# A spectral layer and an ELU network in one kernel: first-layer PSUM by the bank, the B step on 128 rows, and a bias moved

## The chip, the cores and the metric

The kernel runs on one core of one Trainium2 chip. The metric is device time in microseconds (us), the median of several executions. Engines: TensorE (PE in the profile; PEld is its weight load), VectorE (DVE), ScalarE (ACT), GpSimd (POOL) and SyncE (SP), which here only issues transfers.

## The reference

Eight sequences of 3008 rows and 256 columns go through a real Fourier transform along the rows, a complex linear map, a soft threshold, the inverse transform, and then a two-layer network:

```
X = rfft(x, axis=1)                          # Xr, Xi
Yr = Xr @ w_r - Xi @ w_i + b_r
Yi = Xr @ w_i + Xi @ w_r + b_i
Y  = sign(Y) * max(|Y| - 0.01, 0)            # each of Yr, Yi
y  = irfft(Yr + 1j*Yi)                       # 24064 rows x 256
h  = y @ w_in                                # 256 -> 2048
g  = h if h > 0 else exp(min(h, 0)) - 1
out = g @ w_out                              # 2048 -> 256, float32
```

## The kernel before

**The transform.** 3008 = 47 x 64. The forward transform is two sets of matmuls, A (`unit_A`, matrix M1) and X (`unit_X`, matrix M2), the inverse is B (`unit_B`, matrix M3) and Y (`unit_Y`, matrix M4). Between X and B stands M (`unit_M`): the complex map in three real products, its bias and the soft threshold. A sequence has 6 A units, 8 X, 12 M (q from 0 to 5, i 0 and 1), 6 B and 8 Y units. Between A and X, and between B and Y, the data go through DRAM to change their layout (tiles DA, Z, DB, Bs). Each unit of A, X, B and Y fills a pair of PSUM banks (pool psF, one pair) and is copied out by ScalarE or VectorE; M has two banks of its own pool (psM), which takes the place of psF where it is asked for.

**M.** In sequences 2 to 7, k1 (256 columns) is copied to SBUF by VectorE (L295), ps plus that copy is written to yb (L296), and GpSimd adds both biases (L301), clips (L302) and subtracts (L303) into the tile Y: 128 rows, two values of pp, 512 columns. The rows of Y are (s, n2) with s 0 or 1 and 64 values of n2; its columns are (c, d), c the real or imaginary part.

**B.** For each of the two pp, the sum over (c, n2) is made by two matmuls of 64 rows, c 0 and 1, once for each s: eight matmuls of 64 rows and 256 columns a unit.

**The network.** `front(i)` is step i: four matmuls (two halves s of 512 columns, two of the contraction) into the bank pair `hps`, pool psH with two pairs, and ScalarE's Exp of it into Et. `elu` and `finish_elu` make gT, in one of three ways: on "act" steps ScalarE does Relu and Exp of both banks in one pass each (L1024, L1025) and VectorE one pass of 1024 columns (L1048); on "pool" steps ScalarE does Exp by halves (L1022), GpSimd min by halves (L1059) and VectorE L1048 by halves; on the others VectorE does both (L1061, L1050). The pass L1048 reads hps and so gives it back. `back(i)` two steps later multiplies gT by w_out: eight matmuls of 256 columns (L1080) into `ps_o`; every eighth step the sum is copied to osb (L1092) and stored.

**The order.** It is written out by hand. A sequence of the network has 47 steps. `plan(b)` puts the units of the next sequences (A of b+2; X, M, B and the first two Y of b+1; the rest of Y of b) into the steps of b, one unit before a step's front (list f0) or behind it (f1, mostly transfers). `on_act` names the steps of the "act" way, besides all M steps. In the first plan, X starts at step 10. Before step 0 stands a start of some 50 us that does the first sequence's transform with functions of its own (`first_M`, `turn_B`, `split_B`).

All transfers but those of x and w_out are issued by SP, in the order of the program; an issue waits for its operands at the head of that queue.

Of the kernel before, what the change touches and what calls it, by code (L numbers as in the profile page):

```python
# [29 lines left out]
def kernel(  # L30
# [28 lines left out]
    M3 = constp.tile([P, K1 // 2, 2, P], BF16, name="M3")  # L59
# [6 lines left out]
    bias_p = constp.tile([P, 2 * D], BF16, name="bias_p")  # L66
# [10 lines left out]
    space = constp.tile([P, 384], BF16, name="space")  # L77
# [26 lines left out]
    Y_of = {}  # L104
    Bz_of = {}
# [122 lines left out]
    def sum_of(dt, ch):  # L228

        return XS[:, 3 * dt + ch] if 3 * dt + ch < 5 else busy[:]  # L230

    def three_weights(c, dt):

        v, r = (w[:, dt, D * c : D * c + D] for w in (wcat_s, wcat_r))
        a, b_ = (r, v) if c else (v, r)
        nc.gpsimd.tensor_tensor(v, a, b_, ALU.subtract)

    mps_of = {}

    def m_group(b, q, i, ps, biased=False):  # L240
        XT = XT_of[b]
        o = (2 * q + i) * P
        todo = [(c, dt) for c in range(2) for dt in range(2)]
        if b == 0:
            todo.sort(key=lambda z: z[1])
        for c, dt in todo:
            nc.tensor.matmul(  # L247
                ps, lhsT=XT[:, dt, c, o : o + P], rhs=(wcat_r, wcat_s)[c][:, dt, :],
                start=(not biased and (c, dt) == (0, 0)), stop=((c, dt) == (1, 1)),
            )  # L250
        if i == 0:
            Y_of[b, q] = wk3.tile([P, 2, 2 * D], BF16, name="Y", tag="Y")
        if biased:
            yb = ps
        else:
            yb = wk3.tile([P, 2 * D], F32, name="yb", tag="yb")[:]
            nc.vector.tensor_tensor(yb, ps, bias_bc[:], ALU.add)
        if (b, q, i) == (0, 2, 0):
            clip = late3.tile([P, 2 * D], F32, name="gT", tag="gT")
        else:  # L260
            clip = wk2.tile([P, 2 * D], F32, name="clip", tag="clip")
        return yb, clip

    def unit_M(b, q, i):
# [8 lines left out]
        if i == 0:  # L273
            Y_of[b, q] = wk3.tile([P, 2, 2 * D], BF16, name="Y", tag="Y")
# [20 lines left out]
        evac(yb[:, D : 2 * D], k1[:, 0:D], True)  # L295
# [5 lines left out]
        nc.gpsimd.tensor_tensor(yb[:], yb[:], bias_bc[:], ALU.add)  # L301
# [61 lines left out]

    def unit_B(b, v, alone=False, on_dve=False, all_dve=False):
# [5 lines left out]
        Bz, Y = Bz_of[b, v // 2], Y_of.pop((b, v))  # L370
        ps = unit_ps("bps", alone)
        for pp in range(2):
            for c in range(2):
                for s in range(2):
                    nc.tensor.matmul(  # L375
                        ps[:, s, pp * D : pp * D + D],
                        lhsT=M3[s * N2 : s * N2 + N2, 2 * v + pp, c, :],
                        rhs=Y[s * N2 : s * N2 + N2, pp, c * D : c * D + D],
                        start=(c == 0), stop=(c == 1),
                    )  # L380
# [8 lines left out]
        if alone:  # L389
            k0 = 4 * v  # L390
            nc.sync.dma_start(
                DB_of[b][k0 : k0 + 4].rearrange("k p d -> p k d"), Bz[:, o : o + 4, :]
            )
        elif b == 1 and v > 3:
# [19 lines left out]
    def split_B(v, ps, on_dve=(False, True), by_half=False):  # L414
# [8 lines left out]
        def half(pp):  # L423
            for c in range(2):
                for s in range(2):
                    nc.tensor.matmul(
                        ps[s][:, pp * D : pp * D + D],
                        lhsT=M3[s * N2 : s * N2 + N2, 2 * v + pp, c, :],
# [25 lines left out]
    def turn_B(v, ts=(0, 1), ps=None, on_dve=False):  # L454
# [11 lines left out]
        for pp in range(2):  # L466
            for dt in ts:
                for c in range(2):
                    for s in range(2):
# [7 lines left out]
                            rhs=M3[s * N2 : s * N2 + N2, 2 * v + pp, c, :].rearrange(  # L477
# [76 lines left out]

    nc.vector.memset(bias_p[:], 0.0)
# [274 lines left out]
    XS = sump.tile([P, 5, 512], BF16, name="XS")  # L830
# [60 lines left out]
    for o, src, sc, bi in ((1, w3, TURN, 0.0), (0, a3, -TURN, hpi[:])):  # L891
        if o == 0:
            nc.scalar.activation(a3[:], w3[:], AF.Abs)
        nc.scalar.activation(
            M3[:, :, 0, o * N2 : o * N2 + N2], src[:], AF.Sin, bias=bi, scale=sc
# [4 lines left out]
        M3[:, :, 1, 0:N2], M3[:, :, 0, N2:P], 2.0, sgb, ALU.mult, ALU.mult  # L900
    )
    nc.vector.scalar_tensor_tensor(
        M3[:, :, 1, N2:P], M3[:, :, 0, 0:N2], -2.0, sgb, ALU.mult, ALU.mult
# [82 lines left out]
    def front(i, third, on_act, halves):  # L986
        blk, fp = divmod(i, NPAIR)
        early = i < FILL
        if early:
# [10 lines left out]
        if i == PER // NPAIR * NPAIR:  # L1000
            todo.sort(key=lambda z: z[2][0])
        Et = late3.tile([P, 2, TB], F32, name="Et", tag="Et")
        E_ = Et[:]
        for s, ft, (b, t0, c0, c1) in todo:
            for dt in range(2):
                nc.tensor.matmul(  # L1006
                    hps[s][:, c0:c1] if early else hps[:, s, c0:c1],
# [4 lines left out]
            if early and (dt, c1) == (1, TB):  # L1012
                nc.scalar.activation(E_[:, s], hps[s][:], AF.Exp)
        if early:
            return hps, Et
        if i == n - 1:
            for h in range(2):
                t = slice(TB // 2 * h, TB // 2 * h + TB // 2)
                nc.scalar.activation(E_[:, :, t], hps[:, :, t], AF.Exp)
        elif halves:  # L1020
            for s in range(2):
                nc.scalar.activation(E_[:, s], hps[:, s], AF.Exp)  # L1022
        elif on_act:
            nc.scalar.activation(E_, hps[:], AF.Relu, scale=-1.0)  # L1024
            nc.scalar.activation(E_, E_, AF.Exp, scale=-1.0)  # L1025
        else:
            nc.scalar.activation(E_, hps[:], AF.Exp)  # L1027
# [3 lines left out]
    np_all = (slice(0, P), slice(0, 2), slice(0, TB))  # L1031

    def parts(i):

        if i == n - 1:
            return [
                (slice(0, P), slice(0, 2), slice(h, h + TB // 2)) for h in (0, TB // 2)
            ]
        return [(slice(0, P), s, slice(0, TB)) for s in range(2)]

    def finish_elu():
        for i, hps, Et, whole, halves in late_elu:
            gT = late3.tile([P, 2, TB], F32R, name="gT", tag="gT")
            for s in parts(i) if halves else (np_all,):
                h = hps[s[1]][:] if i < FILL else hps[s]
                o, e = gT[s], Et[s]
# [7 lines left out]
    def elu(i, hps, Et, on_pool, on_act):  # L1054

        E_ = Et[:]
        if on_pool:
            for s in parts(i):
                nc.gpsimd.tensor_scalar(E_[s], E_[s], 1.0, 0.0, ALU.min, ALU.max)  # L1059
        elif not on_act:  # L1060
            nc.vector.tensor_scalar(E_, E_, 1.0, -1.0, ALU.min, ALU.add)  # L1061
        late_elu.append((i, hps, Et, on_pool or on_act, on_pool))
# [47 lines left out]
    def plan(b):  # L1110
# [10 lines left out]
        ]  # L1121
        if n1 < B:
            if b:
                lead, xs = 0, (3, 6, 9) if b < 3 else (3, 8, 13)
# [6 lines left out]
                if b < 3:  # L1131
                    seq += [("y", 4)] + M(0) + M(1) + [("y", 5), ("B", 0)]
                else:
                    seq += M(0) + [("y", 4)] + M(1) + [("y", 5), ("B", 0)]
                seq += M(2) + [("y", 6), ("B", 1)] + M(3) + [("y", 7), ("B", 2)]
                on_act = [("X", 4), ("X", 7), ("B", 3)] + [("y", u) for u in range(5, 8)]
                if b < 3:
                    on_act += [("A", 0)]
                    seq += M(4) + [("B", 3)] + M(5) + [("A", 0), ("B", 4), ("B", 5)]
                    seq += [("A", u) for u in range(1, 6)]  # L1140
                else:
                    on_act += [("y", 4), ("B", 4)]
                    seq += M(4) + [("B", 3), ("A", 0)] + M(5) + [("B", 4), ("A", 1), ("B", 5)]
                    seq += [("A", u) for u in range(2, 6)] + [None] * (3 if n2 == B else 2)
                seq += [("n", 0), ("n", 1)]
            else:
                lead, seq = FILL, (
                    [u for u in mid if u[0] != "A"]
                    + [("A", 0), ("A", 1), ("A", 2), ("n", 0), ("n", 1)]
                    + [("A", u) for u in range(3, 6)]  # L1150
                )
# [3 lines left out]
        for t, u in enumerate(seq, lead):  # L1155
# [14 lines left out]
            elif u[0] == "A":  # L1170
                if n2 < B:
                    f0[t].append(put("A", n2, u[1]))
            else:
                f0[t].append(put(u[0], n1, *u[1:]))
            if u == ("B", 5):
                f1[t + (b > 0 and n2 < B)] += [
                    (load_Bs, (n1, w, 0, 4 * K1 - 16 * (b == w == 0))) for w in range(4)
                ]
# [3 lines left out]
        if b == 0:  # L1182
# [24 lines left out]
    for i in range(n + LAG):  # L1207
        if i == FILL:
# [3 lines left out]
                    name="psH", bufs=2, space=bass.MemoryType.PSUM, reuse_waits="tile"  # L1212
# [6 lines left out]
        elif i < n:  # L1219
# [16 lines left out]
            h = front(i, third, on_act, pooled)  # L1236
        finish_elu()
        if i < n:
# [12 lines left out]
            if i == n - 2:  # L1251
                early_h = front(n - 1, True, False, True)
# [36 lines left out]
```

## Time and profile before

| what | us |
|---|---|
| runs | 895.38, 894.95, 894.54; median 894.95 |
| the profiled execution: its span, first to last instruction (the page gives no other time of it) | 903.9 |
| mean granted TensorE clock, share of full speed | 0.948 |
| GpSimd's additions of the biases, L301 | 92.3 in 72 instructions |
| B's matmuls, L375 | 336, mean record 274 ns |
| first-layer matmuls of 512 columns, L1006 into hps | 1240, mean record 390 ns |

The profiled execution is 1.0% longer than the median of the runs. Records of matmuls overlap, as each lasts until its result is out; how fast TensorE goes is read from one start to the next. Idle time of other engines costs nothing unless TensorE then waits for them.

### The profile page before, as it was taken

What the parts mean: (1) busy time and instruction counts of PE and PEld (TensorE: products, weight loads), DVE (VectorE), ACT (ScalarE), POOL (GpSimd) and SP (SyncE); (2) the same over time, 40 slices, a digit from 0 to 9 for tenths busy, and PEclk for the clock granted to TensorE, in tenths of its full rate; (3) what the DMA queues carried; (4) which work ended last, traced back from release to release, by engine and by line L of the source; (5) the groups of instructions that cost most, each with busy time, mean ns of one, the idle gap of its engine ahead of it and who ended that gap; (6) DMA issues with size and microseconds to landing.
All of it is one profiled execution on the core that took longest, in us unless ns stands there. A gap on an engine that the chain in (4) does not pass through costs nothing.

```text
span 903.9 us, 18292 instructions
## 1 busy us (share of the span) xinstructions
PE 891.3 (99%) x6917; PEld 675.2 (75%) x6917; DVE 679.6 (75%) x969; ACT 722.4 (80%) x1001; POOL 596.7 (66%) x806
## 2 busy tenths in 40 slices
PE   9999999999999999999999999999999999999997
PEld 3467667877788777877778777787777877777776
DVE  7788778688866887668866788677876678778776
ACT  6778778888978889798887988878887798776654
POOL 7562550788657886588756877559875697753664
PEclk9999999999999999999999999999999999999998
DMA  8996226631474115632265231643218201241111
GB/s 262 310 258 188 70 71 181 169 119 47 118 209 124 65 50 152 173 117 88 72 181 136 86 116 48 189 140 101 87 53 229 70 24 48 69 108 36 28 44 47
DMA packets 90718, 105.85 MB, mean 117 GB/s; under 512 B 5395, under 2 KB 81174, under 8 KB 87302
## 3 DMA queue, kind: packets, MB, share of 16 engines
q1 hardware_dynamic: 84278, 76.64, 30.0%
q0 software_dynamic: 5968, 27.26, 9.4%
q8 instruction: 54, 0.88, 0.4%
q10 hardware_dynamic: 384, 0.79, 0.3%
q14 instruction: 34, 0.28, 0.1%
HBM read 54.86 MB, written 49.81 MB: 116 GB/s over the span
## 4 chain that ended last, share of the span: by engine, by line
PE 90%; DVE 3%; DMA 3%; ACT 2%; POOL 1%; issue 1%; SPq 0%; DVEq 0%; ACTq 0%; POOLq 0%
PE ps_o L1080 37%; PE hps L1006 36%; PE mps L289 5%; PE bps L375 2%; PE xps L207 2%; PE yps L538 2%; PE aps L170 2%; DVE gT L1048 2%; PE mps L247 1%; DVE Bz L144 1%; DMA xt<-in_x_dram 1%; DMA Z<-DA 1%; DMA DB<-Bz 1%; PE sps L1006 1%; DMA DA<-A 0%
## 5 line engine op out<-in xcount | busy, mean ns | idle before, releaser
L1048 DVE SCALAR_TENSOR_TENSOR gT<-Et,hps 128x512 fp32r<-128x512 f32 (+1 forms) x544 | 423.7, 811 | 158.5 <-POOL Et L1059 115.4
L1080 PE MATMUL ps_o<-w_out_r,gT 128*128 128x256 f32 x3008 | 481.4, 303 | 0.0
L1080 PEld LDWEIGHTS ps_o<-w_out_r,gT 128*128 128x128 f32 x3008 | 407.7, 190 | 52.4 <-ACT osb L1092 0.5
L1059 POOL TENSOR_SCALAR Et<-Et 128x512 f32<-128x512 f32 x434 | 258.3, 614 | 223.6 <-ACT Et L1022 213.2
L1006 PE MATMUL hps<-yT,w_in_s 128*128 128x512 bf16 (+7 forms) x1688 | 388.9, 360 | 2.0 <-DVE gT L1048 1.3
L1022 ACT ACTIVATE Et<-hps 128x512 f32<-128x512 f32 x412 | 224.2, 598 | 67.8 <-PE hps L1006 63.3
L1006 PEld LDWEIGHTS <-w_in_s 128*128 128x128 bf16 x1728 | 144.7, 99 | 119.7 <-issue 21.7
L1024 ACT ACTIVATE Et<-hps 128x1024 f32<-128x1024 f32 x130 | 133.6, 1027 | 57.3 <-PE hps L1006 49.0
L1025 ACT ACTIVATE Et<-Et 128x1024 f32<-128x1024 f32 x130 | 137.4, 1057 | 4.1
L301 POOL TENSOR_TENSOR yb<-yb,bias_bc 128x512 f32<-128x512 f32 x72 | 92.3, 1282 | 9.5 <-DVE yb L296 9.4
L303 POOL TENSOR_TENSOR Y<-yb,clip 128x512 bf16<-128x512 f32 x72 | 92.6, 1286 | 6.0
L296 DVE TENSOR_TENSOR yb<-mps,yb 128x512 f32<-128x512 f32 x72 | 49.8, 692 | 7.6 <-PE hps L1006 0.5
L146 ACT CAST XT<-xps 128x768 bf16<-128x768 f32 x57 | 45.5, 799 | 9.8 <-PE xps L207 9.7
L146 ACT CAST A<-aps 128x1024 bf16<-128x1024 f32 x40 | 40.5, 1014 | 11.4 <-PE aps L170 9.9
L302 POOL TENSOR_SCALAR clip<-yb 128x512 f32<-128x512 f32 x72 | 44.2, 614 | 6.3
L289 PE MATMUL mps<-wcat_s,XT 128*128 128x256 bf16 x288 | 44.1, 277 | 0.0
L144 DVE COPY yb<-mps 128x256 f32<-128x256 f32 x72 | 30.3, 421 | 11.1 <-PE mps L289 9.7
L1050 DVE SCALAR_TENSOR_TENSOR gT<-hps,Et 128x1024 fp32r<-128x1024 f32 x29 | 35.5, 1223 | 2.4
L224 POOL TENSOR_TENSOR XS<-XT 128x512 bf16<-128x512 bf16 x30 | 34.1, 1159 | 2.1 <-ACT XT L146 1.2
L1092 DVE COPY osb<-ps_o 128x512 f32<-128x512 f32 x46 | 31.6, 686 | 1.2 <-PE ps_o L1080 0.5
L146 ACT CAST Bz<-bps 128x1024 bf16<-128x1024 f32 x32 | 31.9, 998 | 0.5 <-PE bps L375 0.4
L1027 ACT ACTIVATE Et<-hps 128x1024 f32<-128x1024 f32 x29 | 29.8, 1029 | 2.6 <-PE hps L1006 1.2
(184 smaller groups left out, 678.8 us busy)
## 6 DMA issues: line engine op xcount, KB each, us to landing
xt<-in_x_dram POOLq DMA_DIRECT2D x21, 1024.0 KB, 5.4
out_dram<-osb SPq DMA_DIRECT2D x158, 128.0 KB
Bs<-DB SPq DMA_DIRECT2D x30, 384.0 KB
DB<-Bz SPq DMA_DIRECT2D x20, 512.0 KB
DA<-A SPq DMA_DIRECT2D x19, 512.0 KB
Z<-DA SPq DMA_DIRECT2D x5, 1152.0 KB
Z<-DA SPq DMA_DIRECT2D x11, 384.0 KB
xt<-in_x_dram POOLq DMA_DIRECT2D x6, 512.0 KB, 6.0
```

The source lines that it names most:

```text
L146: nc.scalar.copy(dst, src)
L289: nc.tensor.matmul(out_, lhsT=lhs[:, dt] if lhs is not None else sum_of(dt, ch)[:, oc : oc + P], rhs=w[:, dt, :], start=(dt == 0), stop=(d ...
L296: nc.vector.tensor_tensor(yb[:].rearrange("p (c d) -> p c d", c=2), ps[:].rearrange("p (c d) -> p c d", c=2), yb[:, D : 2 * D].unsqueeze(1 ...
L301: nc.gpsimd.tensor_tensor(yb[:], yb[:], bias_bc[:], ALU.add)
L303: nc.gpsimd.tensor_tensor(Y_of[b, q][:, i, :], yb[:], clip[:], ALU.subtract)
L1006: nc.tensor.matmul(hps[s][:, c0:c1] if early else hps[:, s, c0:c1], lhsT=w_in_s[:, dt, ft * P : ft * P + P], rhs=yT_of[b][:, dt, t0 : t0 + ...
L1022: nc.scalar.activation(E_[:, s], hps[:, s], AF.Exp)
L1024: nc.scalar.activation(E_, hps[:], AF.Relu, scale=-1.0)
L1025: nc.scalar.activation(E_, E_, AF.Exp, scale=-1.0)
L1048: nc.vector.scalar_tensor_tensor(o, e, -1.0, h, ALU.add, ALU.max)
L1059: nc.gpsimd.tensor_scalar(E_[s], E_[s], 1.0, 0.0, ALU.min, ALU.max)
L1080: nc.tensor.matmul(po[q][:, i_ % 2, :], lhsT=gT[:, s, i_ * P : i_ * P + P], rhs=w_out_r[:, ft, :], start=(ft == 0 and i_ % 2 == 0), stop=( ...
```

## The change

- **First layer.** `hps` becomes two tiles of one bank each (psH: four tiles of a bank). ScalarE's and VectorE's passes L1024, L1025, L1027, L1048 and L1050 go by halves everywhere. The extra pair that idle stretches use comes from psM in place of psF, except for the last step.
- **B.** M3 is kept as two tiles M3[0], M3[1] for the start only and regrouped by four transfers into M3x with rows (c, n2) (`turn_M3`, step 6). After the second M unit of each q, four transfers of 64 rows bring Y to Yx with rows (c, n2) (`turn_Y`), and a B unit is four matmuls of 128 rows without accumulation. Y and Yx share four buffers of pool wk4.
- **M.** b_r is added in the copy of k1; `three_weights` makes b_i - b_r, and GpSimd then adds that to the second half only.
- **Ways and order.** Of the "act" steps beside M, X 4 and X 7 stay; B, Y and A steps go the "pool" way, and their copies to ScalarE. B 0 comes behind M 2, B 5 earlier or later by some steps; the four loads of Bs that follow B 5 are spread over five steps; in the first plan the A units go between the B units, and the first Y unit (n 0) stands three steps behind B 5.
- bias_p moves into a buffer of Bs, `space` shrinks.

```diff
-    M3 = constp.tile([P, K1 // 2, 2, P], BF16, name="M3")
+    M3x = constp.tile([P, K1 // 2, 2, P], BF16, name="M3x")
...
+        if c == dt == 0:
+            b_r_, b_i_ = (bias_bc[:, D * k : D * k + D] for k in range(2))
+            nc.gpsimd.tensor_tensor(b_i_, b_i_, b_r_, ALU.subtract)
...
-        evac(yb[:, D : 2 * D], k1[:, 0:D], True)
+        nc.vector.tensor_tensor(yb[:, D : 2 * D], k1[:, 0:D], bias_bc[:, 0:D], ALU.add)
...
-        nc.gpsimd.tensor_tensor(yb[:], yb[:], bias_bc[:], ALU.add)
+        nc.gpsimd.tensor_tensor(
+            yb[:, D : 2 * D], yb[:, D : 2 * D], bias_bc[:, D : 2 * D], ALU.add
+        )
...
+    def by_part(dst, of):
+        for c in range(2):
+            for s in range(2):
+                nc.sync.dma_start(dst[c * N2 : c * N2 + N2, :, s, :], of(c, s))
+    def turn_M3():
+        by_part(M3x, lambda c, s: M3[c][s * N2 : s * N2 + N2])
+    def turn_Y(b, q):
+        Y = Y_of.pop((b, q))
+        Yx_of[b, q] = Yx = wk4.tile([P, 2, 2, D], BF16, name="Yx", tag="Y")
+        by_part(Yx, lambda c, s: Y[s * N2 : s * N2 + N2, :, c * D : c * D + D])
...
         for pp in range(2):
-            for c in range(2):
-                for s in range(2):
-                    nc.tensor.matmul(
-                        ps[:, s, pp * D : pp * D + D],
-                        lhsT=M3[s * N2 : s * N2 + N2, 2 * v + pp, c, :],
-                        rhs=Y[s * N2 : s * N2 + N2, pp, c * D : c * D + D],
-                        start=(c == 0), stop=(c == 1),
-                    )
+            for s in range(2):
+                nc.tensor.matmul(
+                    ps[:, s, pp * D : pp * D + D], lhsT=M3x[:, 2 * v + pp, s, :],
+                    rhs=Yx[:, pp, s, :], start=True, stop=True,
+                )
...
+        elif last:
+            pair = last_banks("psF").tile([P, 2, TB], F32, name="hps", tag="fps")
+            hps = [pair[:, s, :] for s in range(2)]
         elif third:
-            hps = last_banks("psF").tile([P, 2, TB], F32, name="hps", tag="fps")
+            hps = two_banks(last_banks("psM"), "mps")
         else:
-            hps = psH.tile([P, 2, TB], F32, name="hps", tag="hps")
+            hps = two_banks(psH, "hps")
...
+            left[s] -= 1
+            if left[s] or last:
+                continue
+            if on_act:
+                nc.scalar.activation(Et[:, s], hps[s], AF.Relu, scale=-1.0)
+            else:
+                nc.scalar.activation(Et[:, s], hps[s], AF.Exp)
+        if on_act:
+            for s in range(2):
+                nc.scalar.activation(Et[:, s], Et[:, s], AF.Exp, scale=-1.0)
...
-                on_act = [("X", 4), ("X", 7), ("B", 3)] + [("y", u) for u in range(5, 8)]
+                on_act = [("X", 4), ("X", 7)]
...
+            if u[0] == "M" and u[2] == 1:
+                f1[t].append((turn_Y, (n1, u[1])))
             if u == ("B", 5):
-                f1[t + (b > 0 and n2 < B)] += [
-                    (load_Bs, (n1, w, 0, 4 * K1 - 16 * (b == w == 0))) for w in range(4)
-                ]
+                for w, k in enumerate((0, 2, 3, 4)):
+                    f1[t + k].append((load_Bs, (n1, w, 0, 4 * K1 - 16 * (b == w == 0))))
...
+            f1[6].append((turn_M3, ()))
...
-                    name="psH", bufs=2, space=bass.MemoryType.PSUM, reuse_waits="tile"
+                    name="psH", bufs=4, space=bass.MemoryType.PSUM, reuse_waits="tile"
```

More of the change, by code (lines that the diff above doesn't have):

```diff
@@ L104 @@
     Y_of = {}
+    Yx_of = {}
+    M3 = []
+    XS_of = []
     Bz_of = {}
@@ L228, in sum_of @@
     def sum_of(dt, ch):
-        return XS[:, 3 * dt + ch] if 3 * dt + ch < 5 else busy[:]
+        if 3 * dt + ch == 5:
+            return busy[:]
+        if not XS_of:
+            XS_of.append(sump.tile([P, 5, 512], BF16, name="XS", tag="XS"))
+        return XS_of[0][:, 3 * dt + ch]
     def three_weights(c, dt):
@@ L393, in unit_B @@
             )
-        elif b == 1 and v > 3:
+        elif b == 1 and v > 1:
             nc.sync.dma_start(
@@ L553, in idle_pe @@
             nc.tensor.matmul(ips[:], lhsT=busy[:, 0:P], rhs=busy[:], start=True, stop=True)
+    bias_p = wk4.tile([P, 2 * D], BF16, name="bias_p", tag="Bs")
     nc.vector.memset(bias_p[:], 0.0)
@@ L984, in pieces, with front @@
         return out_
-    def front(i, third, on_act, halves):
+    def front(i, third, on_act):
         blk, fp = divmod(i, NPAIR)
-        early = i < FILL
-        if early:
+        last = i == n - 1
+        if i < FILL:
             hps = two_banks((psS0, psS1)[i % 2], "sps")
+        elif last:
+            pair = last_banks("psF").tile([P, 2, TB], F32, name="hps", tag="fps")
+            hps = [pair[:, s, :] for s in range(2)]
         elif third:
-            hps = last_banks("psF").tile([P, 2, TB], F32, name="hps", tag="fps")
+            hps = two_banks(last_banks("psM"), "mps")
         else:
-            hps = psH.tile([P, 2, TB], F32, name="hps", tag="hps")
+            hps = two_banks(psH, "hps")
+        hps = [h if last else h[:] for h in hps]
         todo = []
@@ L1006, in front @@
                 nc.tensor.matmul(
-                    hps[s][:, c0:c1] if early else hps[:, s, c0:c1],
+                    hps[s][:, c0:c1],
                     lhsT=w_in_s[:, dt, ft * P : ft * P + P],
@@ L1011, in front, with parts @@
                 )
[L1012 to L1016, printed above, removed]
+            left[s] -= 1
[8 more added lines that the diff above has]
+                nc.scalar.activation(Et[:, s], Et[:, s], AF.Exp, scale=-1.0)
+        if last:
             for h in range(2):
                 t = slice(TB // 2 * h, TB // 2 * h + TB // 2)
[L1019 to L1027, printed above, removed]
+                nc.scalar.activation(Et[:, :, t], pair[:, :, t], AF.Exp)
+            hps = pair
         return hps, Et
     late_elu = []
-    np_all = (slice(0, P), slice(0, 2), slice(0, TB))
-    def parts(i):
+    def parts(i, hps, Et):
         if i == n - 1:
-            return [
-                (slice(0, P), slice(0, 2), slice(h, h + TB // 2)) for h in (0, TB // 2)
-            ]
-        return [(slice(0, P), s, slice(0, TB)) for s in range(2)]
+            for h in (0, TB // 2):
+                t = slice(h, h + TB // 2)
+                yield t, slice(0, 2), hps[:, :, t], Et[:, :, t]
+        else:
+            for s in range(2):
+                yield slice(0, TB), s, hps[s], Et[:, s]
     def finish_elu():
-        for i, hps, Et, whole, halves in late_elu:
+        for i, hps, Et, whole in late_elu:
             gT = late3.tile([P, 2, TB], F32R, name="gT", tag="gT")
-            for s in parts(i) if halves else (np_all,):
-                h = hps[s[1]][:] if i < FILL else hps[s]
-                o, e = gT[s], Et[s]
+            for t, s, h, e in parts(i, hps, Et):
+                o = gT[:, s, t]
                 if whole:
@@ L1054, in elu @@
     def elu(i, hps, Et, on_pool, on_act):
-        E_ = Et[:]
         if on_pool:
-            for s in parts(i):
-                nc.gpsimd.tensor_scalar(E_[s], E_[s], 1.0, 0.0, ALU.min, ALU.max)
+            for t, s, h, e in parts(i, hps, Et):
+                nc.gpsimd.tensor_scalar(e, e, 1.0, 0.0, ALU.min, ALU.max)
         elif not on_act:
-            nc.vector.tensor_scalar(E_, E_, 1.0, -1.0, ALU.min, ALU.add)
-        late_elu.append((i, hps, Et, on_pool or on_act, on_pool))
+            nc.vector.tensor_scalar(Et[:], Et[:], 1.0, -1.0, ALU.min, ALU.add)
+        late_elu.append((i, hps, Et, on_pool or on_act))
     def back(i, split):
```

55 lines of the change are left out of this document (25 added, 30 removed), and 8 rows, old and new, of the table mid.

## The prediction

> **What bounds the kernel now.** I read the page first: engine totals, then the chain that ended last.
>
> ```profile
> PE 891.3 (99%) x6917; PEld 675.2 (75%) x6917; DVE 679.6 (75%) x969; ACT 722.4 (80%) x1001; POOL 596.7 (66%) x806
> ...
> PE 90%; DVE 3%; DMA 3%; ACT 2%; POOL 1%; issue 1%; SPq 0%; DVEq 0%; ACTq 0%; POOLq 0%
> ...
> L301 POOL TENSOR_TENSOR yb<-yb,bias_bc 128x512 f32<-128x512 f32 x72 | 92.3, 1282 | 9.5 <-DVE yb L296 9.4
> ```
>
> TensorE is the bound, so a change pays only through what TensorE itself does or waits for. "99% busy" hides waits, because records of consecutive matmuls overlap: one of 512 columns lasts 390 ns, but starts follow at 223 ns. So I measured from start to start in the timeline of PE. A stretch with a B unit (L375) and an M unit (L289):
>
> ```profile
> 198.79 1.29 PE L1080 MATMUL ps_o<-w_out_r,gT 128*128 128x256 f32 x8
> 200.01 0.62 PE L375 MATMUL bps<-Y,M 64*128 64x256 bf16 x8
> 200.56 1.06 PE L1006 MATMUL hps<-yT,w_in_s 128*128 128x512 bf16 x4
> 201.26 1.29 PE L1080 MATMUL ps_o<-w_out_r,gT 128*128 128x256 f32 x8
> 202.39 0.39 PE L289 MATMUL mps<-wcat_r,XS 128*128 128x256 bf16 x2
> 202.62 0.61 PE L289 MATMUL mps<-wcat_s,XT 128*128 128x256 bf16 x4
> 203.07 1.06 PE L1006 MATMUL hps<-yT,w_in_s 128*128 128x512 bf16 x4
> ```
>
> Eight L1080 matmuls take 1.22 us up to B's first (198.79 to 200.01) and 1.13 up to M's (201.26 to 202.39). B's eight take 0.55; M's six take 0.68, 0.113 each. All 42 B units look so; the last L1080 matmul before one lasts 208 to 215 ns to the next start, not 117, and B's last pair 207, not 110.
>
> The second loss stands in the chain in order of time. VectorE copies B's result, then does the 1024-column L1048, and only then does TensorE start the next first-layer group:
>
> ```profile
> 452.14 0.58 PE bps L375 x8
> 452.71 0.03 issue
> 452.74 1.01 DVE Bz L144
> 453.75 0.13 issue
> 453.88 1.22 DVE gT L1048
> 455.10 0.04 issue
> 455.14 1.05 PE hps L1006 x4
> ```
>
> The list of waits has little of it, since the matmul before is still on record:
>
> ```profile
> PE hps L1006 <- DVE gT L1048: 1.3, 3, 0.5
> PEld L1006 <- issue: 21.7, 88, 0.6
> ```
>
> From start to start, against the lower quartile of the same pair of neighbours, 39 L1006 matmuls after 66 us begin over 70 ns late and 41 to 47 ns after a VectorE instruction (L1048, twice L1050) gave the bank pair back: 6.7 us, the longest two 0.68 and 0.69.
>
> **The change, part by part.**
>
> *B on 128 rows.* Pairs of 64-row matmuls start 3 to 4 ns apart, so they already run side by side: eight take the streaming time of four, and halving their number saves none of it. What goes is what surrounds them. Taking M's rate, a unit costs 4 x 0.113 = 0.45 in place of 0.55, and the L1080 group before it 1.13 in place of 1.22: 0.19 us a unit, 42 units, 7.9 us. The Trainium skill, "TensorEngine Tiling (Array Packing)", Key Properties, says that tiles of rows work in parallel and that a change of tiling mode drains the array. The trace agrees with both, 3 ns inside a pair and about 0.09 us at each end of a unit; the page's speedup of 2 alone would have promised nothing for this edit. The ends that I keep: 0 (the loss at the ends comes from something that stays) and 8.3 (0.20 a unit).
>
> *Two tiles of a bank for the first layer.* The first half can be refilled when VectorE has done with 512 columns. Two 512-column L1048 start 0.60 apart, one of 1024 takes 1.21, so the first bank is free about 0.6 us earlier; 36 of the 39 waits are under 0.25 us. The three longer ones are 0.42 with an osb copy ahead on VectorE, which stays, and 0.68 and 0.69 with B copies there, which move to ScalarE. I take 6.0 of 6.7 as gained; ends 0 and 6.7.
>
> The price is more instructions. In an M step ScalarE does Relu and Exp in two passes each: L1022 pairs start 0.49 apart, so 4 x 0.49 = 1.96, against 2.12 now for L1024 and L1025, the second of which waits for the first. VectorE does 0.34 + 0.61 + 2 x 0.60 = 2.15. The step lasts 2.51 (200.56 to 203.07), so both still fit, and this costs 0.
>
> *b_r in the copy pass, GpSimd's min.* The L144 copy of 256 columns (0.42) becomes an add of the same size, and add and copy of 512 columns cost VectorE the same here (692 and 686 ns): 0. L301 halves, 1.28 to an estimated 0.64 to 0.75: GpSimd's M unit falls from 3.17 to about 2.6 against the step's 2.51. It gains 48 L1059 passes of 614 ns (29 us) and loses about 42: no more loaded, only spread differently. A late GpSimd makes y, B and A steps late two steps on; a B step holds it 1.15 of 2.3 us, so it catches up, cost 0. ScalarE takes back 33 copies (22 of yT at 0.79, 9 of Bz and 2 of A at 1.0) and loses the Relu passes there, net about +5 us on 722, hidden under TensorE.
>
> *Regrouping Y.* 42 x 4 transfers of 64 KB on SP's queue, each unit of four waiting for GpSimd's Y. Behind them in SP's order stand output stores and B's stores; two osb buffers cover the former for 16 steps. GpSimd waits in its turn for the first regroups when it writes Y of q = 2, three steps or more later, with the min passes of the next steps behind it: the first regroup should have landed by then (8.0 us after its M unit's start, as worked below, against 7.5 to that step and 2.5 more to the write). B waits for the landing. Worked for the tightest, B 5 of the first plan, four steps after M (5, 1): that unit's matmuls start at 131.10, its Y is written at 135.03, 3.9 later; four issues of 0.4 make 1.6; the wait of a Bs load for B's store averages 2.1 us (22.9 over 11) beyond the issue, so I take 2.5 to land (bounds 2.2 and 4.8). That is 8.0, up to 10.3; four steps of 2.45 are 9.8. So 0, at worst 0.5, once. All others have five steps or more, 12 us. In the same plan n 0 now comes three steps after B 5 (7.3 us): store at +1.8 at the latest, load about 2.5 after that, 2.5 to land, some 6.8; with the slow store seen here (4.5) 8.6. I charge 0.5 for it and 0.5 for the regroup.
>
> *The rest* (M3x built by four transfers at step 6, 17 steps before its first use; bias_p in a Bs buffer; Bs loads one to a step) lies beside work that is not late: 0, bounds 0 and 1 us.
>
> Sum: -7.9 - 6.0 + 1.0 = -12.9 us on the profiled execution's 903.9, which is the only time that the page gives for it. The runs' median is 0.990 of that, so -12.8 on 894.95: **882.2 us**.
>
> **Rivals.**
>
> 1. *The waits for the banks only change place.* ScalarE at 80% is the busiest behind TensorE, and X steps with Relu hold it 0.69 + 1.96 = 2.65 of 2.2 us. If the halves come as late as the pair did, only B's gain is left: 7.9 - 1 = 6.9, 888. For it: X4 and X7 still take the Relu way. Against: X5 and X6 hold ScalarE 1.67 of 2.2.
> 2. *B saves nothing*, because its first matmul now waits for landings of four transfers and the weight load isn't drawn forward. Then 6.0 - 1 = 5.0, 890. Against: the first X unit and Y units wait for transfers too and show 117 to 125 ns ahead of them, as M's do.
> 3. *Slower: regrouped Y comes late.* SP works in order, GpSimd's chain of an M pair grows late by a unit (2.6), and a transfer lands after 5.4 us as those of xt do: 3.9 + 2.6 + 1.6 + 5.4 = 13.5 against five steps of 2.45, 12.2. B 3, B 4 and B 5 would wait 1.3 us in six plans, and B 5 of the first 3.7: 27 us, and -12.9 + 27 gives 909. It decides from 0.31 us of lateness at each of the 42 units (12.9 / 42). Against: the transfers are eight times smaller than xt's, and the queues are lightly used in these stretches (DMA share 0.3 between 167 and 245 us).
>
> **How the numbers follow.** Forecast 0.60, rival 1 0.17, rival 2 0.09, rival 3 0.10, neither better nor worse 0.04. The forecast's own spread is 879 (8.3 + 6.7 + nothing new) to 886. To take in rivals 1 and 2, the range is 878 to 890.5. Faster by over 0.2% (1.8 us, about what a measurement can tell): 0.86; within 0.2%: 0.04; slower 0.10.
>
> **What would show it.** In the profile after: L1080 groups ahead of B at 1.13 and B's four matmuls at 0.45 to 0.46 from start to start; no L1006 start 40 ns after an L1048 end; the first matmul of B without a wait for Yx; GpSimd about 585 us busy, VectorE and ScalarE within 10 us of now. Wrong, if PE has idle time ended by a landing of Yx or Bs, or if the L1080 group ahead of B stays at 1.22.

## The result and the profile after

| kernel | runs, us | median | ratio to before, 95% interval |
|---|---|---|---|
| before | 894.54 to 895.38, 4 runs | 895.15 | |
| changed | 877.67, 881.66, 880.17, 878.72 | 879.44 | 0.9829 [0.9812, 0.9846] |
| changed, again in a later comparison | 877.84 to 878.69, 5 runs | 878.01 (before there: 894.49) | 0.9819 [0.9806, 0.9832] |

The changed kernel is faster by 15.7 us (16.5 in the later comparison). The forecast was 882.2, with 878 to 890.5 as its range.

The page of the changed kernel, to be held against the three lines of before:

```profile
PE 859.0 (98%) x6645; PEld 670.4 (77%) x6749; DVE 668.1 (76%) x1105; ACT 713.6 (81%) x1256; POOL 587.1 (67%) x855
...
PE 87%; POOL 4%; DVE 2%; ACT 2%; DMA 2%; issue 1%; SPq 0%; DVEq 0%; POOLq 0%; ACTq 0%
...
L310 POOL TENSOR_TENSOR yb<-yb,bias_bc 128x256 f32<-128x256 f32 x72 | 53.2, 739 | 11.2 <-DVE yb L305 11.2
```

TensorE is still the bound; the 168 matmuls that B no longer issues are the difference between 6917 and 6749 weight loads. (The trace lacks some hundred matmul records, so PE's own count is lower; they show as gaps of one matmul's length in a stream and are no waits.) The bias pass L310 took 739 ns in place of 1282, at the upper end of the estimate of 0.64 to 0.75 us.

**The two spans on the pages can't be compared.** The profiled execution of before had a granted clock of 0.948 and a span of 903.9 us; that of the changed kernel 0.998 and 875.9. Every later execution of either, and of the variants below, had 0.994 to 1.0. So I profiled the kernel before once more (one run, 895.13 us): 0.999, span 893.2. A run's time is its span and 1.7 to 2.1 us. From here on "before" in a comparison of rows is this second profile. In its timeline of PE, a B unit (L375) and the first-layer matmuls around it:

```profile
196.47 1.28 PE L1080 MATMUL ps_o<-w_out_r,gT 128*128 128x256 f32 x8
197.68 0.61 PE L375 MATMUL bps<-Y,M 64*128 64x256 bf16 x8
198.23 1.04 PE L1006 MATMUL hps<-yT,w_in_s 128*128 128x512 bf16 x3
```

and the same view of the changed kernel, where B is L399, the first layer L1034, the second L1106, and M L298:

```profile
213.15 1.27 PE L1106 MATMUL ps_o<-w_out_r,gT 128*128 128x256 f32 x8
214.27 0.61 PE L399 MATMUL bps<-Yx,M3x 128*128 128x256 bf16 x4
214.72 1.03 PE L1034 MATMUL hps<-yT,w_in_s 128*128 128x512 bf16 x4
215.39 1.29 PE L1106 MATMUL ps_o<-w_out_r,gT 128*128 128x256 f32 x8
216.53 0.28 PE L298 MATMUL mps<-wcat_r,XS 128*128 128x256 bf16 x1
```

From one start to the next, before took 1.21 us for the eight L1080 matmuls and 0.55 for B; after takes 1.12 and 0.45. The group ahead of B now lasts nearly as long as that ahead of M (215.39 to 216.53, 1.14).

The detour of the chain that the prediction showed, from B's matmuls over VectorE's copy of their result and its L1048 to the next first-layer group, is gone. The chain of the changed kernel in order of time, at a B unit of about the same time:

```profile
447.89 0.92 PE ps_o L1106 x8
448.81 0.45 PE bps L399 x4
449.26 0.86 PE hps L1034 x4
```

TensorE follows itself there. What is left of waits, by the profile's list:

```profile
PE hps L1034 <- DVE gT L1075: 1.0, 2, 0.8
PE yps L560 <- DMA Bs<-DB: 0.7, 1, 0.7
```

As that list hides what lies beside a record that is still open, I made the prediction's count again for every kernel, a little wider: each start of a matmul after 75 us that is over 50 ns later than the lower quartile of its pair of neighbours and stands directly behind a release. This is called *lateness* below. The second row of the changed kernel is the profile of its later comparison (e8_after).

| kernel | lateness, us | of it hps behind VectorE | the rest, above all |
|---|---|---|---|
| before, profile at clock 0.948 | 7.6 | 6.6 | |
| before, at 0.999 | 11.8 | 10.2 | osb copies 1.1 |
| changed | 3.1 | 1.6 | n 0 waiting for Bs 0.8 |
| changed, again | 2.7 | 1.6 | n 0 0.5 |

### The profile page after: what moved, and what is told of

The parts are those of the page before. It is cut to its first block, busy times and chain, and to the rows that moved or that the text cites. A ratio compares the mean times of both kernels' runs of the same rounds, so it can differ in the third digit from the quotient of the medians.

```text
span 875.9 us, 18353 instructions
## 1 busy us (share of the span) xinstructions
PE 859.0 (98%) x6645; PEld 670.4 (77%) x6749; DVE 668.1 (76%) x1105; ACT 713.6 (81%) x1256; POOL 587.1 (67%) x855
## 4 chain that ended last, share of the span: by engine, by line
PE 87%; POOL 4%; DVE 2%; ACT 2%; DMA 2%; issue 1%; SPq 0%; DVEq 0%; POOLq 0%; ACTq 0%
PE ps_o L1106 37%; PE hps L1034 31%; PE mps L298 5%; PE mps L1034 2%; PE aps L172 2%; PE xps L209 2%; PE bps L399 2%; PE yps L560 2%; PE mps L256 1%; POOL Y L314 1%; DVE gT L1075 1%; PE sps L1034 1%; POOL Et L1085 1%; DMA Z<-DA 1%; POOL yb L310 1%
## 5 line engine op out<-in xcount | busy, mean ns | idle before, releaser
L1075 DVE SCALAR_TENSOR_TENSOR gT<-Et,hps 128x512 fp32r<-128x512 f32 x610 | 390.2, 683 | 135.6 <-POOL Et L1085 125.7
L1106 PE MATMUL ps_o<-w_out_r,gT 128*128 128x256 f32 x3008 | 476.8, 301 | 0.0
L1106 PEld LDWEIGHTS ps_o<-w_out_r,gT 128*128 128x128 f32 x3008 | 404.0, 189 | 48.1 <-DVE osb L1118 0.2
L1085 POOL TENSOR_SCALAR Et<-Et 128x512 f32<-128x512 f32 x482 | 288.0, 617 | 208.5 <-ACT Et L1046 207.0
L1034 PE MATMUL hps<-yT,w_in_s 128*128 128x512 bf16 (+6 forms) x1491 | 349.9, 351 | 5.6 <-DVE gT L1075 1.0
L1046 ACT ACTIVATE Et<-hps 128x512 f32<-128x512 f32 x494 | 271.5, 609 | 38.6 <-PE hps L1034 34.9
L1034 PEld LDWEIGHTS <-w_in_s 128*128 128x128 bf16 x1728 | 144.0, 98 | 105.1 <-issue 13.1
L1044 ACT ACTIVATE Et<-hps 128x512 f32<-128x512 f32 x192 | 104.5, 597 | 41.8 <-PE hps L1034 32.6
L1049 ACT ACTIVATE Et<-Et 128x512 f32<-128x512 f32 x192 | 110.5, 632 | 0.0
L310 POOL TENSOR_TENSOR yb<-yb,bias_bc 128x256 f32<-128x256 f32 x72 | 53.2, 739 | 11.2 <-DVE yb L305 11.2
L148 ACT CAST XT<-xps 128x768 bf16<-128x768 f32 x57 | 45.8, 805 | 14.6 <-PE xps L209 14.5
L148 ACT CAST yT<-yps 128x752 bf16<-128x752 f32 x56 | 44.1, 788 | 14.5 <-PE yps L560 14.5
L1077 DVE SCALAR_TENSOR_TENSOR gT<-hps,Et 128x512 fp32r<-128x512 f32 x78 | 50.2, 686 | 3.3
L148 ACT CAST Bz<-bps 128x1024 bf16<-128x1024 f32 x41 | 41.6, 1014 | 5.3 <-PE bps L399 4.9
L304 DVE TENSOR_TENSOR yb<-mps,bias_bc 128x256 f32<-128x256 f32 x72 | 30.5, 424 | 17.3 <-PE mps L298 15.5
L298 PE MATMUL mps<-wcat_s,XT 128*128 128x256 bf16 x288 | 43.3, 273 | 0.0
```

Of the source, the lines that this page charges most:

```text
L148: nc.scalar.copy(dst, src)
L298: nc.tensor.matmul(out_, lhsT=lhs[:, dt] if lhs is not None else sum_of(dt, ch)[:, oc : oc + P], rhs=w[:, dt, :], start=(dt == 0), stop=(d ...
L310: nc.gpsimd.tensor_tensor(yb[:, D : 2 * D], yb[:, D : 2 * D], bias_bc[:, D : 2 * D], ALU.add)
L1034: nc.tensor.matmul(hps[s][:, c0:c1], lhsT=w_in_s[:, dt, ft * P : ft * P + P], rhs=yT_of[b][:, dt, t0 : t0 + c1 - c0], start=(dt == 0), sto ...
L1044: nc.scalar.activation(Et[:, s], hps[s], AF.Relu, scale=-1.0)
L1046: nc.scalar.activation(Et[:, s], hps[s], AF.Exp)
```

## The experiments

In the expectations, theory 1 is the prediction's account (TensorE's time at the ends of the B units, and the banks that come back late), theory 2 that the gain is only a higher granted clock, and theory 3 that it comes from copies and steps leaving VectorE and from the new order. The runs of the kernel before beside them had medians of 894.74, 894.39 and 894.49 us.

### The kernel before, profiled again (e0_before)

No edit. 

> The kernel of before once more, for a profile at the clock at which the timed runs went (0.997 to 1.0; the profile that the prediction read was granted 0.948). Theory 1 (what TensorE loses at B units and at late banks is in both): 0.19 us more a B unit than an M unit, and the late starts behind L1048 add up to 7 us or more, since TensorE streams 5% faster and the other engines do not. Theory 2 (clock): span and times differ from the changed kernel's only as the clock does.

Measured: 895.13 us, span 893.2 at clock 0.999. Theory 2 is out: at the same clock the spans differ by 17.3 us (893.2 and 875.9), and the runs by 15.7.

### B on 64 rows again (e1_b64)

```diff
-            for s in range(2):
-                nc.tensor.matmul(... lhsT=M3x[:, 2 * v + pp, s, :], rhs=Yx[:, pp, s, :], ...)
+            for c in range(2):
+                for s in range(2):
+                    nc.tensor.matmul(... lhsT=M3[c][s * N2 : s * N2 + N2, 2 * v + pp, :],
+                        rhs=Y[s * N2 : s * N2 + N2, pp, c * D : c * D + D], ...)
...
-                f1[t].append((turn_Y, (n1, u[1])))
-            f1[6].append((turn_M3, ()))
```

> The changed kernel with B back on pairs of 64-row matmuls out of Y (eight a unit, M3 not regrouped, no transfers from Y to Yx); all else as changed. Theory 1 (TensorE is the bound; the switch to 64 rows and back costs 0.19 us a unit; the first layer's banks are worth 6): 42 x 0.19 = 7.9 back, 887 us. Theory 2 (the gain is a higher granted clock, since the changed kernel's profile shows 0.998 and that of before 0.948): the clock decides, 879 at a clock near 1, whatever B does. Theory 3 (the gain comes from the copies moved off VectorE and the new order, B is worth nothing): 879 to 880.

Measured: 884.39 us, 0.9883 [0.9867, 0.9898]; span 882.2, against 875.9 and 876.2 with B on 128 rows. Its timeline of PE:

```profile
213.70 1.27 PE L1109 MATMUL ps_o<-w_out_r,gT 128*128 128x256 f32 x8
214.91 0.61 PE L400 MATMUL bps<-Y,M3x 64*128 64x256 bf16 x8
215.45 1.04 PE L1037 MATMUL hps<-yT,w_in_s 128*128 128x512 bf16 x4
```

1.21 and 0.54 are back. The medians over all 42 units are 1.223 and 0.543, the same as before's to the nanosecond, and 1.116 and 0.447 after: 0.203 us a unit, 8.5 us. By means, which hold the late starts inside (1.216 and 0.543 here, 1.124 and 0.455 after), it is 0.180 and 7.6. The time moved by less, 5.0 us against the four runs of the changed kernel beside the prediction and 6.4 against the later five: this kernel also has no regroup, and its lateness is 0.9 us against 3.1 and 2.7. The expectation's 887, which charged nothing for the regroup, was 2.6 too high.

### First-layer passes of 1024 columns on one pair tile (e2_onepass)

```diff
-            hps = two_banks(psH, "hps")
+            hps = psH.tile([P, 2, TB], F32, name="hps", tag="hps")
...
-                    name="psH", bufs=4, space=bass.MemoryType.PSUM, reuse_waits="tile"
+                    name="psH", bufs=2, space=bass.MemoryType.PSUM, reuse_waits="tile"
...
+            nc.scalar.activation(E_, hps[:], AF.Relu, scale=-1.0)
+            nc.scalar.activation(E_, E_, AF.Exp, scale=-1.0)
```

VectorE's passes are those of before too, and the extra pair comes from psF again. 

> The changed kernel with the first layer as before: a pair of banks as one tile, ScalarE and VectorE in one pass of 1024 columns on act steps, extra pair from psF. Theory 1: the late starts come back except the two behind B's copies on VectorE, which stay on ScalarE: 4 to 6 us, 884 to 885. Theory 3: 880, since the copies stay on ScalarE and B, Y and A steps on the pool way. Theory 2: 879 at a clock near 1.

Measured: 888.58 us, 0.9925 [0.9913, 0.9937]; lateness 13.1, of which hps 10.1. Undoing the first layer's part costs 9.1 us, more than the 6.0 of the prediction. This run doesn't tell which half of the edit counts, the tiles or the shorter passes.

### One pair tile with passes by halves (e3_pair), a miss

```diff
-            hps = two_banks(psH, "hps")
+            pair = psH.tile([P, 2, TB], F32, name="hps", tag="hps")
+            hps = [pair[:, s, :] for s in range(2)]
```

> The changed kernel with all passes by halves, but the two banks one tile again, so that a pair is given back when the second half is done. Tells the giving back apart from the length of the passes. Theory 1: the release by the bank is what counts, 883 to 885, as in the one-pass kernel. If the shorter passes alone shorten the chain of ScalarE and VectorE enough: 880.

Measured: 1260.92 us. It measured something else. In the changed kernel ScalarE's first pass over the first half (L1048, Exp; on "act" steps L1046, Relu) is issued between the two halves' matmuls; on one tile, the second half's matmuls then wait for that pass. The list of waits:

```profile
PE hps L1036 <- ACT Et L1048: 259.4, 269, 1.8
PE hps L1036 <- ACT Et L1046: 68.5, 96, 1.0
```

These are 328 of the 381 us. What it does show: the early pass on ScalarE is possible only because the halves are two tiles.

### One pair tile, the Exps behind all four matmuls (e11_pair_after)

```diff
+            pair = psH.tile([P, 2, TB], F32, name="hps", tag="hps")
+            hps = [pair[:, s, :] for s in range(2)]
...
-            if left[s] or last:
+            if left[s] or last or i >= FILL:
                 continue
+            nc.scalar.activation(Et[:, s], hps[s], AF.Exp)
```

The extra pair comes from psF again here too. 

> The changed kernel with the first layer's two halves in one tile of two banks (psH: two tiles of a pair) in the 376 steps; ScalarE and VectorE still work by halves, and both Exps stand behind the step's four matmuls, so that they do not stand between them as in the earlier run of a pair by halves (1261). Theory 1 (the gain of the two tiles is that the first bank comes back one 512-column pass, 0.6 us, before the second): late starts behind L1048 as with passes of 1024 columns, 8 to 10 us more than now, 885 to 889 us. Rival (the gain is from the shorter passes and the earlier Exp on ScalarE, not from the release of a bank): 879 to 882.

Measured: 889.36 us, 0.9939 [0.9925, 0.9952], beside 878.01 for the changed kernel: 11.4 us, above the 8 to 10 that theory 1 gave and far from the rival's 879 to 882. Its list of waits has

```profile
PE hps L1036 <- DVE gT L1079: 1.9, 7, 0.5
```

and from start to start its lateness is 12.3 us, of which hps behind VectorE 9.6 in 52 places. The passes of 512 columns alone bring nothing (889.36 here, 888.58 with those of 1024 in e2_onepass): it is the first bank's own release, with the earlier Exp that it allows, that pays. Those two were not parted.

### The old order (e6_order)

```diff
-            ("M", 0, 0), ("M", 0, 1), ("M", 1, 0), ("M", 1, 1), ("M", 2, 0), ("M", 2, 1),
-            ("B", 0), ("M", 3, 0), ("M", 3, 1), ("B", 1), ("M", 4, 0), ("M", 4, 1),
-            ("B", 2), ("M", 5, 0), ("M", 5, 1), ("B", 3), ("A", 0), ("B", 4), ("B", 5),
+            ("M", 0, 0), ("M", 0, 1), ("M", 1, 0), ("M", 1, 1), ("B", 0), ("M", 2, 0),
+            ("M", 2, 1), ("B", 1), ("M", 3, 0), ("M", 3, 1), ("B", 2), ("M", 4, 0),
+            ("M", 4, 1), ("B", 3), ("M", 5, 0), ("M", 5, 1), ("B", 4),
...
```

All plans and the loads of Bs go back; B, banks, bias and ways stay. 

> The changed kernel with the order of units and of the Bs loads as before, and the ways as changed: B 5 then stands three steps behind M 5 (two in the first plan), B 0 of the first plan three. Theory 1 with the regroup at 8.0 us: B waits 3.1 + 0.7 in the first plan and about 0.7 to 0.8 in six others, 8 to 9 us, 888; if a regroup lands in 5 us: 880; in 10 us: 900.

Measured: 896.73 us, 1.0021 [1.0007, 1.0035]: without its order the whole change is no gain. The list of waits, and the chain in order of time at B 5 of the first plan:

```profile
PE bps L399 <- DMA Yx<-Y: 13.2, 14, 2.3
```

```profile
131.77 1.29 POOL Y L279
...
133.07 0.59 SPq L379
...
135.01 2.05 DMA Yx<-Y
...
137.11 0.50 PE bps L399 x3
```

M (5, 1) starts at 129.14 and its Y is written at 133.06; four issues on SP follow, 0.6 us each, and the last transfer lands 2.05 after the start of its issue, at 137.06: 7.9 us in all. B 5 stands two steps behind that unit in the first plan, and waits 2.5 and 0.4 us for it. In the six later plans it stands three steps behind and waits 1.8 to 2.7, in two parts each: there Y is written 4.8 to 5.2 us after the unit's start and not 3.9, so that the expectation, which took 8.0 us for all plans, came out too low (888). These seven units make 15.3 of the 16.1 us of lateness behind landings, which is most of the price of the old order (896.73 - 879.44 = 17.3).

The clock adds to it: behind two of these waits, from 137.5 and from 779.2 us, the granted clock was 0.5 for 3.4 us. From the first-layer matmuls there (137.45) to the next unit's start (140.78) TensorE took 3.3 us, where 1.8 is usual, and the second stretch cost as much.

The Trainium skill, "DMA: Bandwidth & Descriptors", Anatomy of one DMA, gives for the GpSimd path a fixed cost of about 2.0 us a transfer and little for 64 KB on top. The 2.05 us measured here are near it, though on SP's queue, another path.

### The old ways (e4_ways)

```diff
-                on_act = [("X", 4), ("X", 7)]
+                on_act = [("X", 4), ("X", 7), ("B", 3)] + [("y", u) for u in range(5, 8)]
+                    on_act += [("A", 0)]
+                    on_act += [("y", 4), ("B", 4)]
```

> The changed kernel with the act steps of before (B 3, y 5 to 7, A 0 or y 4 and B 4 by Relu and Exp on ScalarE, their copies on VectorE). Theory 1: hidden, 879 to 880. Theory 3 (copies off VectorE are what helps): 3 us or more back, 883.

Measured: 878.56 us, 0.9826 [0.9812, 0.9839], the changed kernel's own ratio within the intervals. VectorE has 28.8 us more (696.9), GpSimd 42 less (545.1), and the end doesn't move. Moving these steps is worth nothing in the changed kernel; theory 3 keeps only its order.

### Both biases on GpSimd again (e5_bias)

```diff
-        nc.vector.tensor_tensor(yb[:, D : 2 * D], k1[:, 0:D], bias_bc[:, 0:D], ALU.add)
+        evac(yb[:, D : 2 * D], k1[:, 0:D], True)
...
-        nc.gpsimd.tensor_tensor(
-            yb[:, D : 2 * D], yb[:, D : 2 * D], bias_bc[:, D : 2 * D], ALU.add
-        )
+        nc.gpsimd.tensor_tensor(yb[:], yb[:], bias_bc[:], ALU.add)
```

> The changed kernel with GpSimd adding both biases over 512 columns again, and a plain copy of k1. GpSimd's M unit is then 3.2 us of a step's 2.5 with min passes in between. Theory 1: GpSimd falls behind by 0.6 us an M unit, 1.3 us over a pair, and catches up in the B and y steps; 880. If the moved min passes need the shorter unit: TensorE waits at L1106 behind them, or B waits for Yx, 885 or more.

Measured: 904.0 us, 1.011 [1.0094, 1.0125]. The bias edit, priced at 0, carries 24.6 us in the changed kernel. The list of waits and a piece of the chain:

```profile
PE hps L1029 <- DVE gT L1070: 15.9, 30, 1.8
```

```profile
205.52 1.24 POOL yb L307
...
207.53 1.26 POOL Y L309
208.80 0.59 POOL Et L1080
209.41 0.70 DVE gT L1070
...
210.15 0.59 PE hps L1029 x2
```

GpSimd works through M's passes (L307 to L309), and the min pass of a network step (L1080) stands behind them; VectorE's pass waits for it, and that pass is what gives hps back to TensorE. Lateness of hps: 26 us. GpSimd's share of the span is 69% here.

### Both biases on GpSimd and the old ways (e9_biasways)

The two edits above together. 

> GpSimd adds both biases over 512 columns again, as in the run of that edit alone (904.0), but the Y, B and A steps that were moved to the GpSimd min are back on the way before. Theory 1 (the long bias pass hurts because GpSimd now has both it and about 20 min passes a plan more): GpSimd is relieved of some 40 min passes of 0.61 us, its M chain is in time again, hps waits behind L1048 fall from 26 us to under 6, 879 to 884 us. Rival (it hurts because of the new order, or because hps is needed sooner): the waits stay, 898 to 904. In between, 885 to 897, both have a share, and it is read off from the steps at which hps then waits.

Measured: 886.6 us, 0.9916 [0.9903, 0.993]. Both have a share, as the expectation's middle case: of 24.6 us, 17.4 come with the min passes moved to GpSimd, and 8.0 (886.6 against e4_ways, 878.6) stay without them. For those 8.0 the trace points to the order: six M units, with one Y unit between them (none in the first plan, two from the fourth on), now come ahead of the first B unit, where there were four. With the long pass GpSimd needs 21.0 us for the six (186.28 to 207.27), while TensorE's starts of them lie within 14.5 us (184.54 to 199.03); the min pass behind them is late, and hps with it:

```profile
PE hps L1029 <- DVE gT L1070: 5.3, 4, 2.2
```

Two of these waits, 2.3 and 2.2 us in the first two plans that have such a chain, make most of it. With the short pass and the same ways (e4_ways) the six are done in 17.7 us (186.05 to 203.79). That the order is what makes the short pass needed is supported by one more run: on the old order, with the two tiles of a bank and the long pass (the next run), hps is 2.7 us late in all, here 7.7. Of the 8.0, lateness explains some 6 us against e4_ways (10.4 and 4.2). Another 1.6 are the clock: directly behind the first of the two waits it was granted at 0.5 for 3.4 us, and the timeline of PE has

```profile
208.66 1.87 PE L1029 MATMUL hps<-yT,w_in_s 128*128 128x512 bf16 x4 [2.16 <-DVE gT L1070]
209.96 2.23 PE L1101 MATMUL ps_o<-w_out_r,gT 128*128 128x256 f32 x8
```

with the next unit at 212.03, 3.4 us after 208.66, where 1.8 is usual.

### Only the two tiles of a bank, in the kernel before (e7_onlyP)

```diff
-            hps = psH.tile([P, 2, TB], F32, name="hps", tag="hps")
+            hps = two_banks(psH, "hps")
...
-                    name="psH", bufs=2, space=bass.MemoryType.PSUM, reuse_waits="tile"
+                    name="psH", bufs=4, space=bass.MemoryType.PSUM, reuse_waits="tile"
```

The passes by halves and the extra pair's move to psM come with it; B, bias, ways and order are as before. 

> The kernel of before with the first layer's two tiles of a bank and passes by halves as the only part of the change (the spare bank pair from psM with it). Theory 1 as predicted: 6 us less than before, 889; by the kernel with one pass, which lost 8.6 against the changed one: 886. Theory 3: 893 to 895, since the copies on VectorE are still there.

Measured: 887.16 us, 0.9919 [0.9905, 0.9934], 7.2 us less than before beside it (894.39); lateness falls from 11.8 to 3.5, that of hps from 10.2 to 2.7.

### The changed kernel as a control (e8_after)

> The changed kernel itself, as a control on the same chip as the two beside it. All theories: 877.5 to 882 us, ratio 0.981 to 0.985.

Measured: 878.01 us, 0.9819 [0.9806, 0.9832], as given in the table above.

## Why the prediction was right, point by point

- **What bounds: right.** What was traced of the gains and losses is found in TensorE's start to start times, and taking 29 us off VectorE (from e4_ways to the changed kernel) moved nothing. Rivals 1 (888) and 2 (890) are out: the lateness behind VectorE fell from 10.2 to 1.6, and B on 64 rows costs 5.0 to 6.4 us.
- **B on 128 rows, 7.9: right, by its own rows.** The marks that the prediction set were groups at 1.13 ahead of B and units at 0.45 to 0.46; the trace has 1.124 and 0.455 in the mean, and 7.6 to 8.5 us over the 42 units. The price of 64 rows is about 0.1 us at each end, and no streaming time. The Trainium skill, "TensorEngine Tiling (Array Packing)", Key Properties, says that a change of tiling mode drains the array. The trace agrees: with the change of mode gone, so is the 0.1 us at either end. By the lateness of e1_b64, the regroup takes 1.8 to 2.2 us of the gain back.
- **Two tiles of a bank, 6.0: the mechanism right, the size too small.** It was 8.6 us of lateness (10.2 to 1.6), above the upper end of 6.7; 7.2 to 9.1 in time (e7_onlyP, e2_onepass). The step that failed is the base: the 6.7 were read in an execution at clock 0.948, in which first-layer matmuls start every 224 ns and not every 216, while VectorE is as busy as ever (679.6 and 679.3 us), so that VectorE was late less often. The same program at 0.999 has 10.2 where it had 6.6; that is one profile at each clock. The sign "no L1006 start 40 ns after an L1048 end" did not come in full: 1.6 us of such starts are left.
- **More passes of half the size, 0: right.** VectorE 668.1 and ScalarE 713.6 us busy; the prediction had them within 10 us of 679.6 and 722.4, and VectorE is 11.5 lower, just outside. ScalarE was to grow by some 5 and fell by 9; nothing hung on it.
- **b_r in the copy, min on GpSimd, 0: the sum right, the reasons incomplete.** In the changed kernel the short pass is worth 24.6 us with the min passes on GpSimd and 8.0 without them: it takes away what the new order and those passes would cost, so that the three should come to about 0 together, which was not run by itself. The prediction's "it catches up, cost 0" holds only with the short pass. Total load (587 us, predicted about 585) says nothing on that; the six M units in a row do.
- **Regroup and order.** The worked 8.0 us for the regroup in the first plan stands at 7.9, though two of its parts were off and cancelled: an issue takes 0.6 and not 0.4 us, and the last landing comes 1.5 behind its issue and not 2.5. The 0.5 charged for B 5 did not come: M (5, 1) starts at 125.55 and B 5 at 135.01, 9.5 us later, without a wait. Rival 3 (909) was a real mechanism: with B 5 four steps behind M (5, 1) in the first plan and five in the later ones nothing waits, with two and three (e6_order) 17.3 us are lost. The forecast rests on the order's lead more than the text said; it priced rival 3 by slow transfers, where two steps less lead do it. One step less was not run. One argument against rival 3 was misread: the regroup's transfers (64 KB) are sixteen times smaller than those of xt that land in 5.4 us (1024 KB), not eight.
- **n 0 three steps behind B 5, 0.5:** 0.8 us in one profile, 0.5 in the control, where the list of waits names ScalarE, but a transfer landed 0.135 us ahead of the start, as in the first. So a sign that the prediction gave for being wrong, TensorE idle until a landing of Bs, came, at the price that it had charged. In the first profile the store of B 5 took 2.3 us and the load of Bs 3.2, so n 0 began at 142.65:

```profile
135.17 0.47 PE bps L399 x4
...
136.99 2.29 DMA DB<-Bz
...
139.30 3.22 DMA Bs<-DB
...
142.65 0.49 PE yps L560 x8
```

- **The scale, x 0.990: right in effect, its cause not seen.** The text took the profiled execution as 1% longer than the runs; it was the clock, which stood on the page as 0.948. Scaling a sum of late starts by 0.990 was the wrong use of that: from 0.948 to 0.999 they did not shrink, they grew (7.6 to 11.8).
- **The sum.** At a clock of 0.998 to 1.0: about 8 for B, and lateness down by 8.7 (11.8 to 3.1) or, in the later profile, by 9.1 (to 2.7). That makes 16.7 and 17.1, and the spans are 17.3 and 17.0 us shorter (893.2 to 875.9 and 876.2). The runs show 15.7 and 16.5. The 2.8 us by which the forecast was too high (882.2 against 879.4) are mostly the banks' 2.6. Two side sums of the prediction were off: the forecast's own lower end, given as 879, comes to 880.1 (894.95 less 15.0 x 0.990), and n 0's slow case, given as 8.6, to 8.8 (1.8 + 4.5 + 2.5); nothing hung on either.

No kernel here beats the changed one: e4_ways is equal to it within the intervals.

## What to carry to other kernels

Ahead of any sum of waits, read the granted clock of the profiled execution: where it is lower, the bound engine can be slower and the others seem in time, so that the price of a late release is read too low (6.6 for 10.2 here). An edit that costs nothing in the sum can still be what holds another up; undo each part alone before saying what a change is worth, since here three parts (order, bias, banks) each cost 9 to 25 us when taken out, and together the change is worth 16. A transfer put between two matmul groups is paid in lead: work out its time from the producer's start, count the steps, and give it one more.

## What the runs showed of the hardware that was not expected

- The granted clock was 0.948 in one execution of the kernel before and 0.994 to 1.0 in every other one that lists it, on one core in both cases. It does not slow all matmuls alike: those of 512 bf16 columns start every 224 ns at 0.948 and every 216 at 0.999, M's of 256 bf16 columns 114 and 109 in the median, but the second layer's of 256 columns in fp32 118 and 118. So a clock lower by 5% made the span longer by only 1.2%.
- The clock also drops within an execution. In e6_order (twice) and e9_biasways (once) it was granted at 0.5 for 3.41 us within 1 us of the end of a wait of 2.3 to 2.9 us, and each stretch cost about 1.6 us on top of the wait. After a wait of 2.2 us in e9_biasways (at 318.2) it did not drop; what decides it, these runs don't show. One such stretch lies in the start of e5_bias (from 11.5 us) and one in that of e7_onlyP (from 47.2).
- GpSimd busy for only 69% of the span went with a loss of 24.6 us, as its work comes in rows: six M units, and behind them the min passes for which the first layer waits.
- A transfer of 64 KB within SBUF held SP's queue for 0.6 us an issue in most cases (up to 0.9), so that four of them took 2.5 us ahead of whatever SP had next.
